# Turning cached keys on VectorE in 32x32 blocks instead of on TensorE, in a two-layer decode kernel

## The chip, the cores and the metric

One core of one Trainium2 chip. The metric is the device time of one execution in microseconds (us), lower is better. A single core has no second die to compare with, so a run is called "slow" here only when it lies more than 1.5% above the fastest run of the same kernel; all others are "fast". Ratios use fast runs alone. "Faster" and "slower" mean by more than 2%; a smaller difference is told with its interval (95%).

## The reference, cut to what matters

Four sequences (B = 4) decode one token each through attention, a gated feed-forward block, and then attention and feed-forward again. Both attention blocks read the same key and value caches, with 32 query heads over 8 cached heads, 4096 positions and a head size of 128, in bf16.

```python
def _A_ref(x, k_cache, v_cache, wq, wo):
    q = ...                                   # (B, 32, 1, 128)
    k = jnp.repeat(k_cache, rep, axis=1)      # rep = 4 query heads per cached head
    v = jnp.repeat(v_cache, rep, axis=1)
    scores = jnp.einsum("bhqd,bhkd->bhqk", q, k) * (Dh ** -0.5)
    p = _softmax(scores, axis=-1)
    o = jnp.einsum("bhqk,bhkd->bhqd", p, v)
    return ... @ wo

x = x + _A_ref(_layernorm(x, axis=-1), A_k_cache, A_v_cache, A_wq, A_wo)
x = x + _B_ref(_layernorm(x, axis=-1), B_w_gate, B_w_up, B_w_down)
x = x + _A_ref(_layernorm(x, axis=-1), A_k_cache, A_v_cache, A_wq, A_wo)
x = x + _B_ref(_layernorm(x, axis=-1), B_w_gate, B_w_up, B_w_down)
```

The kernel walks over the sequences. The turned keys of one sequence stay on chip for both layers ("first pass" and "second pass"); the values are loaded twice.

## The kernel before

A key tile arrives with positions on partitions. The score matmuls of this kernel take them with the head dimension there, so TensorE transposes each 128x128 block with an identity matrix into PSUM, and VectorE or ScalarE copies eight blocks at a time back (`keys`). The score matmuls hold the queries still, in slots padded with zeros so that each of eight key blocks writes its own four of 32 PSUM rows (`scores`). The exponential writes its result in the order in which it reads (`softmax`), and the value matmuls take 4 KB runs of the value cache (`values`).

```python
def keys(b, kvh):
    kt = ktp.tile([P, NKB, NCC, P], BF16, name="kt", tag="kt")     # NKB = 8, NCC = 4
    KT[kvh] = kt
    for t in range(2):
        kn = kvin.tile([P, 2, NKB, Dh], BF16, name="k_t", tag="kv")
        rows = slice(t * CH * P, (t + 1) * CH * P)
        dq.dma_start(out=kn.rearrange("p i k d -> p (i k) d"),
                     in_=A_k_cache[b, kvh, rows].rearrange("(p c) d -> p c d", p=P))
        for hi in range(2):
            tp = ps_tp.tile([P, NKB, P], BF16, name="tp", tag="tp")
            for kb in range(NKB):
                nc.tensor.transpose(tp[:, kb, :], kn[:, hi, kb, :], ident_bf[:, :])
            evac(kt[:, :, 2 * t + hi, :], tp[:])      # 3 of 5 on VectorE, 2 of 5 on ScalarE

def scores(g, zq):
    sc = ps_sc.tile([P, NCC * P], FP32, name="sc", tag="sc")
    for kb in range(NKB):
        for s in range(GH):                            # GH = 4 cached heads in a group
            kvh = g * GH + s
            off = ZW * (kvh + 1) - rep * (kb + 1)
            nc.tensor.matmul(sc[ZW * s:ZW * (s + 1), :], lhsT=zq[:, off:off + ZW],
                             rhs=KT[kvh][:, kb].rearrange("p c k -> p (c k)"), ...)

# in softmax(): maximum over the row (VectorE), over the partitions (GpSimd), then
nc.scalar.activation(out=pr.rearrange("p c k -> p (c k)"), in_=sc[:], func=ACT.Exp,
                     bias=nb[:, 0:1], scale=scale, accum_out=ls[:])

def q_turn(qs, g):                                     # queries of the second pass
    qt = ps_tp.tile([P, rep, P], BF16, name="qt", tag="tp")
    for h in range(rep):
        nc.tensor.transpose(qt[:, h, :], qs[:, h, :], ident_bf[:, :])
    nc.vector.tensor_copy(out=zslots(zq2, g * GH, GH),
                          in_=qt.rearrange("p h (k w) -> p k h w", w=ZW)[:, :, :, 0])

# in values(): two tiles a head, 4 KB runs, then 32 matmuls of 4 columns
dq.dma_start(out=v.rearrange("p i k d -> p (i k) d"),
             in_=A_v_cache[b, kvh, rows].rearrange("(p c) d -> p c d", p=P))
```

The kernel keeps TensorE and the one load queue in the order of the program text. The order around the change from sequence b-1 to b, which the document calls "the turn", is:

```python
        q_turn(qs[0], 0)                     # end of sequence b-1
        sc = scores(0, zq2)
        q_turn(qs[1], 1)
        soft2 = [softmax(sc), softmax(scores(1, zq2))]
        # ... next sequence
        keys(b, 0); prob2 = [turn(soft2[0])]
        keys(b, 1); keys(b, 2); prob2.append(turn(soft2[1])); keys(b, 3)
        soft1 = softmax(scores(0, z1))
        keys(b, 4); keys(b, 5); p1 = [turn(soft1)]
        # ... first value matmuls of sequence b, keys 6 and 7, scores(1, z1), ...
```

## Time and profile before

| kernel before | |
|---|---|
| time, median of 3 runs | 355.69 us (355.35 to 357.77) |
| span of the profiled run | 354.5 us |
| busy: TensorE, VectorE, ScalarE | 247.8, 127.4, 66.0 us |
| transposes of keys / their copies | 75.9 us on TensorE / 51.5 us on VectorE and 52.0 on ScalarE |
| bytes moved by the load queue | 114.58 MB |

No single engine fills the span, so this table does not say what a change is worth. The prediction below reads the stages in which the transfers do not run full. Two groups of the page of the kernel before (name, shapes, count, busy us and mean ns, idle time before them and its cause): the score matmuls and the exponential.

```profile
L304 PE MATMUL sc<-kt,zq 128*32 128x512 bf16 x512 | 37.1, 414 | 5.3 <-DVE zq L204 2.1 <-ACT kt L278 1.9 <-DVE kt L280 1.1
L322 ACT ACTIVATE pr<-sc,nb 128x512 bf16<-128x512 f32 x16 | 11.0, 689 | 97.9 <-DVE am L318 97.9
```

And the granted TensorE clock in 40 slices of the span, in tenths of full speed:

```profile
PEclk9869985555699986556999665556998855587555
```

A 5 is half speed. The 9s are the stages in which keys are turned (1.00 from 175 to 190 us), the 5s mostly those in which four-column value matmuls run (0.50 from 209 to 235). Where a trace has no clock record the row shows 9 too; this one has records from 9.4 us on.

### The profile page before, as it was taken

What the parts mean: (1) busy time and instruction counts of PE and PEld (TensorE: products, weight loads), DVE (VectorE), ACT (ScalarE), POOL (GpSimd) and SP (SyncE); (2) the same over time, 40 slices, a digit from 0 to 9 for tenths busy, and PEclk for the clock granted to TensorE, in tenths of its full rate; (3) what the DMA queues carried; (4) which work ended last, traced back from release to release, by engine and by line L of the source; (5) the groups of instructions that cost most, each with busy time, mean ns of one, the idle gap of its engine ahead of it and who ended that gap; (6) DMA issues with size and microseconds to landing.
All of it is one profiled execution on the core that took longest, in us unless ns stands there. A gap on an engine that the chain in (4) does not pass through costs nothing.

```text
span 354.5 us, 12013 instructions
## 1 busy us (share of the span) xinstructions
PE 247.8 (70%) x5444; PEld 200.6 (57%) x5444; DVE 127.4 (36%) x484; ACT 66.0 (19%) x90; POOL 13.4 (4%) x36
## 2 busy tenths in 40 slices
PE   4578651753888687569887776789886677695465
PEld 4576531643366557555766565755766576644455
DVE  6225330130565421214755120333863303153014
ACT  3215220000064320000545200001652300001000
POOL 0000000000010000000100000000000000001000
PEclk9869985555699986556999665556998855587555
DMA  7998999999459999998699989995799999973940
GB/s 279 411 407 279 349 354 389 407 399 375 184 159 337 329 412 383 409 396 291 197 355 350 410 295 406 408 327 196 232 394 368 392 359 411 383 275 129 398 176 2
DMA packets 35747, 115.34 MB, mean 325 GB/s; under 512 B 3176, under 2 KB 9072, under 8 KB 35696
## 3 DMA queue, kind: packets, MB, share of 16 engines
q1 hardware_dynamic: 35696, 114.58, 86.3%
q8 instruction: 42, 0.69, 0.8%
q14 instruction: 9, 0.07, 0.1%
HBM read 114.56 MB, written 0.00 MB: 323 GB/s over the span
## 4 chain that ended last, share of the span: by engine, by line
DMA 39%; PE 34%; DVE 12%; ACT 6%; issue 5%; POOL 2%; SPq 2%; ACTq 0%; POOLq 0%; DVEq 0%
DMA v_t<-in_A_v_cache_dram 18%; DMA k_t<-in_A_k_cache_dram 10%; PE tp L294 8%; PE sc L304 8%; PE ot L356 7%; DMA wd_sb<-in_B_w_down_dram 6%; DMA wq_sb<-in_A_wq_dram 5%; PE qr L192 4%; ACT kt L278 3%; DVE kt L280 3%; ACT pr L322 3%; PE yT L264 2%; DVE m L311 2%; PE hu L256 1%; SPq L351 1%
## 5 line engine op out<-in xcount | busy, mean ns | idle before, releaser
L356 PE MATMUL ot<-pT,v_t 128*128 128x4 bf16 x2048 | 69.8, 166 | 48.2 <-DMA v_t<-in_A_v_cache_dram 36.8
L356 PEld LDWEIGHTS <-v_t 128*128 128x128 bf16 x2048 | 63.7, 103 | 57.9 <-DMA v_t<-in_A_v_cache_dram 42.0
L294 PE MATMUL tp<-ident_bf,k_t 128*128 128x128 bf16 x1024 | 75.9, 236 | 13.2 <-DMA k_t<-in_A_k_cache_dram 7.5
L294 PEld LDWEIGHTS <-k_t 128*128 128x128 bf16 x1024 | 67.8, 107 | 21.1 <-issue 11.0
L278 ACT COPY kt<-tp 128x1024 bf16<-128x1024 bf16 x52 | 52.0, 1012 | 74.2 <-PE tp L294 74.0
L280 DVE COPY kt<-tp 128x1024 bf16<-128x1024 bf16 x76 | 51.5, 688 | 27.6 <-PE tp L294 27.0
L304 PE MATMUL sc<-kt,zq 128*32 128x512 bf16 x512 | 37.1, 414 | 5.3 <-DVE zq L204 2.1
L361 DVE TENSOR_TENSOR OT_bf<-ot,rden 128x4 bf16<-128x4 f32 x64 | 10.1, 158 | 81.0 <-PE ot L356 80.9
L322 ACT ACTIVATE pr<-sc,nb 128x512 bf16<-128x512 f32 x16 | 11.0, 689 | 97.9 <-DVE am L318 97.9
L304 PEld LDWEIGHTS <-zq 128*32 128x32 bf16 x512 | 14.0, 102 | 21.9 <-issue 6.3
L218 PE MATMUL yT<-OT_bf,wo_sb 128*128 128x1 bf16 (+1 forms) x640 | 21.2, 166 | 1.7 <-issue 1.2
L311 DVE TENSOR_REDUCE m<-sc 128x1 f32<-128x512 f32 x16 | 10.8, 676 | 30.9 <-PE sc L304 30.9
L247 ACT ACTIVATE th<-t 128x14 f32<-128x14 f32 (+1 forms) x5 | 1.1, 222 | 109.7 <-DVE t L245 109.7
L218 PEld LDWEIGHTS <-wo_sb 128*128 128x128 bf16 x640 | 19.5, 104 | 1.9 <-issue 1.9
L316 POOL PARTITION_ALL_REDUCE gm<-am x16 | 6.2, 386 | 284.1 <-DVE am L313 268.8
L192 PE MATMUL qr<-wq_sb,xpad 128*32 128x512 bf16 x128 | 13.9, 612 | 0.6 <-DVE msq L152 0.5
L264 PE MATMUL yT<-H_bf,wd_sb 128*128 128x1 bf16 (+1 forms) x280 | 8.3, 166 | 6.9 <-DMA wd_sb<-in_B_w_down_dram 3.6
L338 PE MATMUL ptp<-ident_bf,pr 128*128 128x128 bf16 x64 | 6.8, 235 | 8.5 <-ACT pr L322 8.0
L264 PEld LDWEIGHTS <-wd_sb 128*128 128x128 bf16 x280 | 8.0, 104 | 7.1 <-DMA wd_sb<-in_B_w_down_dram 3.7
L256 PE MATMUL hu<-xc_bf,wu_sb 128*128 128x1 bf16 (+1 forms) x280 | 8.5, 165 | 4.8 <-DMA wu_sb<-in_B_w_up_dram 2.9
L256 PEld LDWEIGHTS <-wu_sb 128*128 128x128 bf16 x280 | 8.0, 104 | 5.0 <-DMA wu_sb<-in_B_w_up_dram 3.0
L338 PEld LDWEIGHTS <-pr 128*128 128x128 bf16 x64 | 4.5, 103 | 9.7 <-ACT pr L322 8.9
(65 smaller groups left out, 123.6 us busy)
## 6 DMA issues: line engine op xcount, KB each, us to landing
v_t<-in_A_v_cache_dram SPq DMA_DIRECT2D x128, 512.0 KB, 7.0
k_t<-in_A_k_cache_dram SPq DMA_DIRECT2D x64, 512.0 KB, 5.6
wq_sb<-in_A_wq_dram SPq DMA_DIRECT2D x2, 2048.0 KB, 13.0
wo_sb<-in_A_wo_dram SPq DMA_DIRECT2D x1, 4096.0 KB
wg_sb<-in_B_w_gate_dram SPq DMA_DIRECT2D x1, 1792.0 KB, 11.1
wu_sb<-in_B_w_up_dram SPq DMA_DIRECT2D x1, 1792.0 KB, 15.2
wd_sb<-in_B_w_down_dram SPq DMA_DIRECT2D x1, 1792.0 KB, 20.0
x_bf<-in_A_x_dram SPq DMA_DIRECT2D x1, 4.0 KB
```

Source lines behind the costliest of these rows:

```text
L192: nc.tensor.matmul(qr[ZW * j:ZW * (j + 1), :], lhsT=xpad[:, k, :], rhs=wq_sb[:, k, c0:c0 + rep * Dh], start=(k == 0), stop=(k == KD - 1), ...
L218: nc.tensor.matmul(OP["y"][:, :, dk], lhsT=wo_sb[:, i, dk * P:(dk + 1) * P], rhs=o_bf[:, bs, i], start=(i == 0 and dk == 0), stop=(i == Hq ...
L256: nc.tensor.matmul(hu[:, m, :], lhsT=wu_sb[:, k, m * P:(m + 1) * P], rhs=xc_bf[:, bs, k], start=(k == 0), stop=(k == KD - 1))
L264: nc.tensor.matmul(yT[:, :, dk], lhsT=wd_sb[:, k, dk * P:(dk + 1) * P], rhs=H_bf[:, k, :], start=(k == 0), stop=(k == KF - 1))
L278: nc.scalar.copy(out=out_ap, in_=in_ap)
L280: nc.vector.tensor_copy(out=out_ap, in_=in_ap)
L294: nc.tensor.transpose(tp[:, kb, :], kn[:, hi, kb, :], ident_bf[:, :])
L304: nc.tensor.matmul(sc[ZW * s:ZW * (s + 1), :], lhsT=zq[:, off:off + ZW], rhs=KT[kvh][:, kb].rearrange("p c k -> p (c k)"), start=(kb == 0) ...
L311: nc.vector.tensor_reduce(out=m[:], in_=sc[:], axis=AX.X, op=ALU.max)
L322: nc.scalar.activation(out=pr.rearrange("p c k -> p (c k)"), in_=sc[:], func=ACT.Exp, bias=nb[:, 0:1], scale=scale, accum_out=ls[:])
L338: nc.tensor.transpose(ptp[:, cc, :], pr[:, cc, :], ident_bf[:, :])
L356: nc.tensor.matmul(ot[:], lhsT=v[:, hi, kb, :], rhs=pT[:, 2 * t + hi, c:c + rep], start=(t == 0 and hi == 0 and kb == 0), stop=(t == 1 and ...
```

## The change

The intent: take the full transposes, with their two trips through PSUM, away. The new kernel has VectorE transpose within 32x32 blocks directly from SBUF to SBUF. Two bf16 numbers are taken as one four-byte element, so that one instruction turns a whole 512 KB half head (128x1024 elements). What comes out, by the index arithmetic of the code, is not a full transpose: each group of 32 partitions holds 32 of the pairs of head dimensions for its own positions. The queries make up for it: they are spread block-diagonally over the four partition groups (`dsel`, `gmask`, `spread`), so that a score matmul sums only what belongs together. The new order of positions spreads to the rest: the exponential writes with a step of four elements, to bring the positions back into the order that the value matmuls need, and values load in 2 KB runs.

```diff
     def keys(b, kvh):
-        kt = ktp.tile([P, NKB, NCC, P], BF16, name="kt", tag="kt")
+        kt = ktp.tile([P, C, Dh], BF16, name="kt", tag="kt")
+        src = A_k_cache[b, kvh].rearrange("(p a) d -> p a d", p=P)
         for t in range(2):
-            kn = ...; dq.dma_start(...)
-            for hi in range(2):
-                tp = ps_tp.tile([P, NKB, P], BF16, name="tp", tag="tp")
-                for kb in range(NKB):
-                    nc.tensor.transpose(tp[:, kb, :], kn[:, hi, kb, :], ident_bf[:, :])
-                evac(kt[:, :, 2 * t + hi, :], tp[:])
+            kn = kvin.tile([P, CH, Dh], BF16, name="k_t", tag="kv")
+            al = slice(t * CH, (t + 1) * CH)
+            dq.dma_start(out=kn[:], in_=src[:, al])
+            nc.vector.transpose(out=kt[:, al].rearrange("p a d -> p (a d)").bitcast(I32),
+                                in_=kn.rearrange("p a d -> p (a d)").bitcast(I32))
@@ scores
+        for be in range(2):
+            for j in range(NJ):
+                for s in range(GH):
+                    off = (kvh * NJ + j) * ZW + (1 - be) * ZW // 2
+                    kt = KT[kvh].rearrange("p (a b n) (j c o) -> p b j o n a c", a=4, b=2, j=2, o=2)
+                    nc.tensor.matmul(sc[ZW * s:ZW * (s + 1), :], lhsT=zq[:, off:off + ZW],
+                                     rhs=kt[:, be, j // 2, j % 2], ...)
@@ softmax
-        nc.scalar.activation(out=pr.rearrange("p c k -> p (c k)"), in_=sc[:], func=ACT.Exp,
+        nc.scalar.activation(out=pr.rearrange("p n (c a) -> p n a c", a=4),
+                             in_=sc.rearrange("p (n a c) -> p n a c", n=NCC, a=4), func=ACT.Exp,
@@ q_turn
-        nc.vector.tensor_copy(out=zslots(zq2, g * GH, GH), in_=qt.rearrange(...)[:, :, :, 0])
+        qT = grp.tile([P, GH, rep], BF16, name="qT", tag="qT")
+        nc.vector.tensor_copy(out=qT[:], in_=qt.rearrange("p h (k w) -> p k h w", w=ZW)[:, :, :, 0])
+        qz = ps_misc.tile([P, GH, NJ, rep], FP32, name="qz2", tag="misc")
+        for j in range(NJ):
+            nc.tensor.matmul(qz[:, :, j, :], lhsT=dsel[:, j], rhs=qT[:], start=True, stop=True)
+        spread(g * GH, qz.rearrange("p k j h -> p (k j) h"))
@@ values
+        src = A_v_cache[b, kvh].rearrange("(i p l) d -> p i (l d)", i=NI, p=P)
...
+            dq.dma_start(out=v.rearrange("p i b n d -> p i (b n d)"), in_=src[:, 2 * t:2 * t + 2])
```

(Cut: the constants, the same spreading for the first pass, PSUM pools of 3 and 1 buffers that become 2 and 2, a third buffer for the probabilities, the index order in the value matmuls. The order of the stages in the program is unchanged.)

## The prediction

> **What bounds the kernel now.** I read the page first: engine shares, the 40 slices and the queue.
>
> ```profile
> PE 247.8 (70%) x5444; PEld 200.6 (57%) x5444; DVE 127.4 (36%) x484; ACT 66.0 (19%) x90; POOL 13.4 (4%) x36
> ...
> DMA  7998999999459999998699989995799999973940
> GB/s 279 411 407 279 349 354 389 407 399 375 184 159 337 329 412 383 409 396 291 197 355 350 410 295 406 408 327 196 232 394 368 392 359 411 383 275 129 398 176 2
> ...
> q1 hardware_dynamic: 35696, 114.58, 86.3%
> ```
>
> No engine is full; TensorE's 70% counts pipelined matmuls. The hardware queue moves 114.58 MB, and its packets fill 86% of the span. The GB/s row stands near 400 for long stretches and falls in groups of slices: at 88 to 106 us, 159 to 186, 230 to 257 and after 310. At the best rate below, 416 GB/s, the bytes alone take 114.58 / 0.416 = 275 us, so some 80 us are time in which the transfers do not run full. Those holes are what the change can win or widen.
>
> Then the chain that ended last, by engine and by line:
>
> ```profile
> DMA 39%; PE 34%; DVE 12%; ACT 6%; issue 5%; POOL 2%; SPq 2%; ACTq 0%; POOLq 0%; DVEq 0%
> DMA v_t<-in_A_v_cache_dram 18%; DMA k_t<-in_A_k_cache_dram 10%; PE tp L294 8%; PE sc L304 8%; PE ot L356 7%; DMA wd_sb<-in_B_w_down_dram 6%; DMA wq_sb<-in_A_wq_dram 5%; PE qr L192 4%; ACT kt L278 3%; DVE kt L280 3%; ACT pr L322 3%; PE yT L264 2%; DVE m L311 2%; PE hu L256 1%; SPq L351 1%
> ```
>
> Transfers are the largest part, values first. The key path (transposes 8%, their copies out of PSUM 3% on ScalarE and 3% on VectorE) is 14%, about 50 us. That is the most this change could ever take away.
>
> Then stretches of one batch's period (72 to 75 us from one block of query projections to the next): the columns are length, busy time and count per engine, granted TensorE clock, transfer share, GB/s.
>
> ```profile
> 161.00:175.00 14.00, 12.72 (x202) 7.40 (x202) 7.85 (x32) 2.67 (x4) 1.21 (x3) 0.81 0.77 262
> 175.00:190.00 15.00, 12.81 (x213) 10.39 (x211) 10.32 (x23) 9.47 (x13) 1.27 (x3) 1.00 0.96 332
> 190.00:209.00 19.00, 13.25 (x236) 9.77 (x235) 5.66 (x16) 3.83 (x6) 0.83 (x2) 0.78 0.95 361
> 209.00:235.00 26.00, 18.84 (x618) 17.90 (x616) 5.07 (x34) 0.22 (x1) 0.00 (x0) 0.50 0.97 377
> ```
>
> 161 to 175 is the turn from one batch to the next (second-pass queries, two score groups, two softmaxes): 262 GB/s. 175 to 190 turns the next batch's keys. 209 to 235 is the value stretch: 377 GB/s, TensorE at half clock, VectorE 5 of 26 us busy. Only transfers bound that last one.
>
> The turn in order of time, from the chain (start, length, what):
>
> ```profile
> 165.81 0.46 PE qt L203 x4
> 166.30 0.19 DVE zq L204
> ...
> 166.53 1.94 PE sc L304 x32
> 168.49 0.69 DVE m L311
> ...
> 173.47 0.61 PE tp L294 x8
> ...
> 181.47 1.30 DVE kt L280 x2
> ...
> 182.82 1.90 PE sc L304 x29
> ```
>
> After the scores at 166.53, transposes for the new batch wait until the second score group is through, and eight key tiles pass until scores start again at 182.82. Key slots bind them: eight transposed heads are held, all in use until the scores have read them. Six load buffers stand full meanwhile, and the queue has nothing to issue into. So in the turn the transfer rate is the rate at which key tiles are turned.
>
> [...] The trace before has one such operation, the last row here (names, shapes, count, busy us and mean ns):
>
> ```profile
> L280 DVE COPY kt<-tp 128x1024 bf16<-128x1024 bf16 x76 | 51.5, 688 | 27.6 <-PE tp L294 27.0
> ...
> L278 ACT COPY kt<-tp 128x1024 bf16<-128x1024 bf16 x52 | 52.0, 1012 | 74.2 <-PE tp L294 74.0
> ...
> L196 DVE TENSOR_SCALAR qs<-qr,rstd 128x512 bf16<-128x512 f32 x8 | 6.0, 751 | 4.2 <-PE qr L192 4.2
> ...
> L86 DVE STREAM_TRANSPOSE irow<-icol 128x32 f32<-128x32 f32 x1 | 0.2, 205 | 0.0
> ```
>
> [...] a stretch of 1 KB rows (output weights) and one of 4 KB rows (keys and values), both with the transfer share full, ran at
>
> ```profile
> 48.00:55.00 7.00, 0.82 (x13) 0.20 (x5) 1.63 (x7) 0.78 (x2) 0.83 (x2) 0.91 1.09 348
> ...
> 125.00:129.00 4.00, 3.78 (x54) 2.97 (x55) 1.39 (x2) 2.02 (x2) 0.00 (x0) 0.57 1.02 416
> ```
>
> 348 and 416 GB/s. [...] (one score group took 3.61 us at 240.6 and 1.91 at 169.3). The key stretch, 175 to 190, full of transposes, is held at 1.00; without them TensorE will idle there.
>
> **The change part by part.**
>
> Removed: 1024 transposes (75.9 us busy on TensorE) and 128 copies (51.5 us on VectorE, 52.0 on ScalarE).
>
> Added on VectorE: 64 block transposes of 1024 four-byte elements. [...] 1.24 us, an estimate. Sum 79 us. Spreading the queries: a PSUM operation of 512 elements took 751 ns (the qs row), so 0.7 us for each of four batches, and about 0.42 for each of eight half-size ones: 6 us. VectorE goes from 127 to about 127 - 52 + 79 + 6 = 161 us, ScalarE to 14, TensorE to some 175. Averages fit; the question is the turn.
>
> The turn. The instruction order of the new kernel puts a block transpose ahead of the query copy and the maximum of the second group, and others between the softmax steps. From the end of the first scores until eight tiles are turned VectorE must do 8 x 1.24 = 9.9 us plus what stands between: two maxima 1.38, three query operations 1.3, two each of the mask 0.46, the bias 0.5, the row sums 0.48, the reciprocals 0.5 and the probability copies 0.83: 5.5. Together 15.4 us, against 182.82 - 168.47 = 14.4 before. The first tile is free 2.5 us earlier, the eighth about 1 to 2 us later, and tiles 9 to 12 again meet a softmax. VectorE alone replaces three engines that shared the work. Against that, the last key tile of the first layer needs 1.24 us from landing to scores where two blocks of transposes and a 1.02 us copy took 3; but then those scores come after a TensorE pause and run at half clock, 3.5 for 1.9. I call the sum of the key part +0.5 us a period.
>
> Second-pass queries: between the query transposes and the scores there are now a copy, four small matmuls (166 ns of latency each, pipelined, 0.28), another handover and the 0.42 us spread: +0.8 us on the chain in each of four batches. The second group hides behind the first except at the end.
>
> Values. The new key order makes every value run 2 KB instead of 4. Per packet and engine, 16 x 4096 B / 416 GB/s = 157 ns and 16 x 1024 / 348 = 47; a straight line gives 84 ns at 2048 B, 391 GB/s, so a value tile takes 1.34 us for 1.26. All 128 would pay 10 us; where the chain hangs on value landings (about 20 tiles a batch, 210.7 to 226.2 and part of the projections after) it is about 1.7 us a batch. Key runs keep 4 KB.
>
> Sum: three turns at 0.5 + 0.8 + 1.7 = 3.0 make 9. The first batch adds 1 for its scores at half clock (its opening is held by weight transfers until 20.2 us anyway), and the tail 0.8 + 0.4 + 1.2 for queries and values, 3.4 together. That is +12. Since TensorE's in-order queue loses 76 us of work that also delayed value matmuls, which I cannot place on the chain, I take 3 back: 355.7 + 9 = 365.
>
> **The rivals.** (a) The handovers were the bound. If most of the 50 us of the key path vanishes behind landings, 330 to 342. For it: in the queue's own waits, 54.8 us of key loads stood until transposes freed a buffer. Against: in the turn a VectorE tile (1.24 us) is no faster than what TensorE and two copy engines did (14.4 us for eight with the softmaxes in it). (b) Transfers hide everything: the value stretches are 35% of the span and neither kernel changes their bytes; 353 to 359. Against: the packets shrink. (c) [...] 2.3 us a tile, 147 us in all; VectorE would be the bound in the key stretches, +10 us for eight tiles in each turn, 390 to 400. [...] (d) The packets cost in full, near 10 us by themselves, with the turn unchanged: 366.
>
> **Range and chances.** 365 us, 350 to 379 eight times in ten: the lower end lets a third of (a) through beside half of my costs, the upper end allows the full packet cost and 2 us more in each turn. Two per cent are 348.6 and 362.8. Faster 0.20, for the handovers; same 0.33, because the changes are single microseconds in both directions; slower 0.47.
>
> **What would show it.** The block transposes' mean: 1.2 to 1.3 us is my step, over 2 is rival (c). Value stretches with full transfer share: 391 GB/s is the packet step, 410 refutes it. From the end of a batch's second-pass scores to the next batch's first: 15 to 17 us is the turn step; under 12 and I am wrong, since VectorE then overlaps better than its order suggests. Score groups of the first layer at 3.5 us would confirm the clock. ScalarE near 14 and VectorE near 161 us check the counts. If the GB/s row fills in the turn slices and the total falls below 345, rival (a) holds.

The 1.24 us of a block transpose and the 2.3 us of rival (c) are estimates. The trace before, with one block transpose of 32 columns in 205 ns, does not show either.

## The result, and the profile after

| | before | after |
|---|---|---|
| median of 3 runs | 355.69 us | 368.15 us (366.34 to 369.49) |
| ratio of fast runs | | 1.033 (95%: 1.024 to 1.042) |
| profiled span | 354.5 us | 366.3 us |

The change makes the kernel slower by 3.3%. Ratios here and below are the mean time of one kernel's fast runs over that of the other's in the same rounds, so not quite the ratio of the medians quoted.

The page of the changed kernel, with the rows that answer to those shown of before: engines, clock, transfers, queue, and the chain that ended last by engine and by line.

```profile
PE 195.3 (53%) x4468; PEld 140.3 (38%) x4468; DVE 155.0 (42%) x483; ACT 24.8 (7%) x38; POOL 13.4 (4%) x36
...
PEclk9999999999965655555956555558665555586555
DMA  7999799999358999999698999997899999963940
GB/s 276 411 401 355 234 349 375 389 399 379 140 173 267 340 364 330 369 385 350 212 351 319 360 352 362 385 314 262 300 378 326 379 346 385 357 226 119 385 179 4
...
q1 hardware_dynamic: 52080, 114.58, 87.0%
...
DMA 34%; PE 28%; DVE 22%; ACT 7%; issue 6%; POOL 2%; SPq 1%; ACTq 0%; POOLq 0%; DVEq 0%
DMA v_t<-in_A_v_cache_dram 24%; PE sc L320 10%; DVE kt L307 9%; PE ot L374 7%; ACT pr L339 6%; DMA wd_sb<-in_B_w_down_dram 6%; DMA k_t<-in_A_k_cache_dram 4%; PE qr L211 4%; PE yT L287 2%; DVE m L328 2%; POOL den L346 1%; DVE zq L145 1%; PE hu L279 1%; PE st L158 1%; DVE pT L358 1%
```

TensorE lost 52.5 us of busy time and ScalarE 41.2; VectorE gained 27.6. The bytes are the same but the packets are smaller (52080 for 35696). In the chain the transposes and their copies (14% before) have become block transposes (9%), values have grown from 18% to 24%, scores from 8% to 10% and the exponential from 3% to 6%. The clock row needs care. Its first eleven 9s say nothing: this trace has no clock record before 100.9 us, and the two score groups there (23.6 to 31.2 and 47.7 to 51.3 us) have medians of 632 and 628 ns a matmul, as at half clock. From the 12th slice on the row has far fewer 9s than before: the scores' growth has its reason in the clock. For the same cause the mean granted clock of a whole run is not compared here.

The groups concerned:

```profile
L307 DVE STREAM_TRANSPOSE kt<-k_t 128x1024 int32<-128x1024 int32 x64 | 77.5, 1227 | 16.4 <-DMA k_t<-in_A_k_cache_dram 8.4 <-PE sc L320 7.9
...
L320 PE MATMUL sc<-kt,zq 128*32 128x512 bf16 x512 | 52.0, 534 | 18.8 <-DVE kt L307 13.9 <-DVE zq L145 4.8
L339 ACT ACTIVATE pr<-sc,nb 128x512 bf16<-128x512 f32 x16 | 22.4, 1401 | 191.2 <-DVE am L335 144.6 <-DVE OT_bf L379 46.6
...
L145 DVE TENSOR_TENSOR zq<-qz,gmask 128x256 bf16<-128x256 f32 x8 | 3.3, 418 | 1.5 <-PE qz L228 1.3
...
L145 DVE TENSOR_TENSOR zq<-qz,gmask 128x512 bf16<-128x512 f32 x4 | 2.7, 675 | 0.0
```

A block transpose takes 1.23 us. The score matmuls are the same 512 instructions of the same shape as before and take 534 ns where they took 414. Over single matmuls the shortest is 376 ns in both kernels, and the median went from 379 to 628 ns: more of them run at half clock (the group at 208.34 us was granted 0.50 and took 3.56 us, that at 174.01 was granted 1.00 and took 2.01; with 378 and 630 ns for the two kinds, the means come to 14% of them before and 62% after). The new layout of their moving operand adds little: a second-pass group of 32 at full clock took 1.99 to 2.03 us where it took 1.91. The exponential of 128x512 takes 1401 ns for 689. Nothing in the prediction had that.

The turn of the changed kernel in order of time, from the chain (start us, length us, engine and line):

```profile
173.53 0.44 DVE zq L145
...
174.01 2.01 PE sc L320 x26
...
176.08 1.13 issue
177.21 0.13 DVE qT L225
177.35 0.60 DVE m L328
...
178.42 1.15 DVE kt L307
...
187.70 2.28 DVE kt L307 x2
...
190.02 3.39 PE sc L320 x27
...
193.44 0.69 DVE m L328
...
196.73 1.41 ACT pr L339 x2
...
199.62 1.01 PE ot L374 x32
...
200.65 0.16 DVE OT_bf L379
200.81 1.16 DVE kt L307
201.99 5.71 DMA v_t<-in_A_v_cache_dram
...
208.34 3.56 PE sc L320 x32
```

To read it: the first second-pass scores end at 176.03, the copy of the second queries waits 1.13 us for a block transpose that stands ahead of it in VectorE's order, and block transposes then follow each other to the next sequence's scores at 190.02. That is 14.0 us, against 14.35 before (168.47 to 182.82). The key part of the turn has not become longer. But then the first scores take 3.39 for 1.90 us, the maximum and its successors stand between further block transposes, and the exponential takes 1.41: the first value matmul of the new sequence comes at 199.62, 23.6 us after the same starting point, where it came after 21.4 us before (168.47 to 189.89). The line at 208.34 is the second group of first-layer scores, 3.56 us.

What that does to the transfers, in windows cut at the same events (length, busy time and count of TensorE, weight loads, VectorE, ScalarE, GpSimd, then granted clock, transfer share, GB/s). Before:

```profile
168.50:182.80 14.30, 11.91 (x207) 9.60 (x205) 10.10 (x26) 7.53 (x10) 1.65 (x4) 1.00 0.75 243
182.80:189.90 7.10, 6.33 (x98) 4.78 (x99) 4.46 (x11) 4.52 (x6) 0.83 (x2) 1.00 1.03 381
189.90:197.00 7.10, 4.85 (x108) 4.25 (x108) 2.31 (x5) 1.15 (x3) 0.00 (x0) 1.00 0.96 368
```

After, with a value stretch as the last line:

```profile
176.00:190.00 14.00, 5.74 (x91) 3.04 (x88) 13.44 (x27) 2.80 (x4) 1.66 (x4) 0.74 0.78 269
190.00:199.60 9.60, 3.99 (x33) 1.62 (x33) 6.16 (x11) 1.39 (x2) 0.83 (x2) 0.68 0.99 355
199.60:208.30 8.70, 2.49 (x84) 2.37 (x87) 4.98 (x6) 0.00 (x0) 0.00 (x0) 0.50 0.86 303
222.00:233.00 11.00, 6.93 (x201) 6.35 (x202) 2.70 (x19) 0.00 (x0) 0.00 (x0) 0.50 1.04 385
```

In the turn (first lines) the rates are 243 and 269 GB/s, VectorE is busy 13.44 of 14 us after the change, and the clock has fallen from 1.00 to 0.74. Up to the first value matmul (second lines) the queue still fills buffers, 381 and 355 GB/s. Then comes the hole: 199.6 to 208.3 moves 303 GB/s where the same place before moved 368, TensorE is busy 2.49 of 8.7 us, and the chain there says why: it waits 5.71 us for a value tile that was issued at 201.99, when a block transpose had freed a load buffer; this transpose stood in VectorE's order behind the scaling of the first outputs (`OT_bf`, 200.65), which needs the late first value matmuls. Where values run full (last line), they run at 385 GB/s with a transfer share over 1.

### The profile page after: what moved, and what is told of

It is laid out like the page before. It is cut to its first block, busy times and chain, and to the rows that moved or that the text cites.

```text
span 366.3 us, 10014 instructions
## 1 busy us (share of the span) xinstructions
PE 195.3 (53%) x4468; PEld 140.3 (38%) x4468; DVE 155.0 (42%) x483; ACT 24.8 (7%) x38; POOL 13.4 (4%) x36
## 2 busy tenths in 40 slices
DMA packets 52123, 115.22 MB, mean 315 GB/s; under 512 B 3176, under 2 KB 9072, under 8 KB 52080
## 3 DMA queue, kind: packets, MB, share of 16 engines
q1 hardware_dynamic: 52080, 114.58, 87.0%
## 4 chain that ended last, share of the span: by engine, by line
DMA 34%; PE 28%; DVE 22%; ACT 7%; issue 6%; POOL 2%; SPq 1%; ACTq 0%; POOLq 0%; DVEq 0%
DMA v_t<-in_A_v_cache_dram 24%; PE sc L320 10%; DVE kt L307 9%; PE ot L374 7%; ACT pr L339 6%; DMA wd_sb<-in_B_w_down_dram 6%; DMA k_t<-in_A_k_cache_dram 4%; PE qr L211 4%; PE yT L287 2%; DVE m L328 2%; POOL den L346 1%; DVE zq L145 1%; PE hu L279 1%; PE st L158 1%; DVE pT L358 1%
## 5 line engine op out<-in xcount | busy, mean ns | idle before, releaser
L307 DVE STREAM_TRANSPOSE kt<-k_t 128x1024 int32<-128x1024 int32 x64 | 77.5, 1227 | 16.4 <-DMA k_t<-in_A_k_cache_dram 8.4
L320 PE MATMUL sc<-kt,zq 128*32 128x512 bf16 x512 | 52.0, 534 | 18.8 <-DVE kt L307 13.9
L339 ACT ACTIVATE pr<-sc,nb 128x512 bf16<-128x512 f32 x16 | 22.4, 1401 | 191.2 <-DVE am L335 144.6
L320 PEld LDWEIGHTS <-zq 128*32 128x32 bf16 x512 | 16.7, 118 | 43.5 <-issue 33.2
L356 PE MATMUL ptp<-ident_bf,pr 128*128 128x128 bf16 x64 | 9.1, 291 | 39.2 <-ACT pr L339 39.2
L328 DVE TENSOR_REDUCE m<-sc 128x1 f32<-128x512 f32 x16 | 10.9, 683 | 26.5 <-PE sc L320 26.5
L343 DVE TENSOR_SCALAR lm<-onehot,ls 128x16 f32<-128x16 f32 x16 | 3.7, 231 | 16.4 <-ACT pr L339 16.3
L200 PE MATMUL qps<-xc_bf,wq_sb 128*128 128x4 bf16 x128 | 3.7, 168 | 11.6 <-DMA wq_sb<-in_A_wq_dram 11.6
L260 PE MATMUL hg<-xc_bf,wg_sb 128*128 128x1 bf16 (+1 forms) x280 | 8.2, 165 | 2.6 <-DMA wg_sb<-in_B_w_gate_dram 2.2
L260 PEld LDWEIGHTS <-wg_sb 128*128 128x128 bf16 x280 | 8.1, 105 | 2.8 <-DMA wg_sb<-in_B_w_gate_dram 2.2
```

Of the source, the lines that this page charges most:

```text
L260: nc.tensor.matmul(hg[:, m, :], lhsT=wg_sb[:, k, m * P:(m + 1) * P], rhs=xc_bf[:, bs, k], start=(k == 0), stop=(k == KD - 1))
L307: nc.vector.transpose(out=kt[:, al].rearrange("p a d -> p (a d)").bitcast(I32), in_=kn.rearrange("p a d -> p (a d)").bitcast(I32))
L328: nc.vector.tensor_reduce(out=m[:], in_=sc[:], axis=AX.X, op=ALU.max)
L339: nc.scalar.activation(out=pr.rearrange("p n (c a) -> p n a c", a=4), in_=sc.rearrange("p (n a c) -> p n a c", n=NCC, a=4), func=ACT.Exp, ...
L356: nc.tensor.transpose(ptp[:, cc, :], pr[:, cc, :], ident_bf[:, :])
```

## The experiments

Three theories of the 3.3%: (1) the exponential's strided write, about 0.7 us for each of 16 softmaxes; (2) the value runs of 2 KB; (3) score groups at half clock, 3.56 us each for 1.90 (that this comes of TensorE having less to do before them is a guess). The rival to all of them is the new part itself: VectorE's block transposes and the longer path of the queries, now in one engine's order.

Each kernel ran beside the kernel before on the same chip; there were three calls on three chips, of 5, 3 and 5 rounds. The changed kernel itself ran again only in the first, so what the second and third say against it is a comparison across chips. Kernels marked "wrong" compute something else; they still passed the tolerance, since with these inputs attention is nearly uniform over 4096 positions. That the kernels called correct are so rests on the index arithmetic of their code.

| kernel | ratio to before, 95% | median us | before |
|---|---|---|---|
| changed kernel again (after_again) | 1.036 (1.031 to 1.041) | 367.30 | 354.35 |
| exponential written in order (exp_flat) | 1.020 (1.010 to 1.030) | 364.34 | 354.35 |
| values in 4 KB runs (v_4k) | 1.024 (1.018 to 1.029) | 363.18 | 354.35 |
| filler matmuls (pe_warm) | 1.060 (1.055 to 1.066) | 375.10 | 354.35 |
| first-layer scores halved (score_half) | 1.020 (1.006 to 1.033) | 362.18 | 358.64 |
| short query path (query_short) | 1.031 (1.017 to 1.044) | 366.52 | 358.64 |
| three undone (three_undone) | 0.989 (0.977 to 1.000) | 351.53 | 358.64 |
| exponential reads strided (exp_read) | 1.025 (1.013 to 1.037) | 364.81 | 358.64 |
| before, 2 KB values (before_v2k) | 1.014 (1.009 to 1.019) | 358.42 | 354.33 |
| before, strided exponential (before_exp) | 1.023 (1.017 to 1.030) | 363.45 | 354.33 |
| mended | 1.025 (1.019 to 1.032) | 363.26 | 354.33 |
| mended_more | 1.011 (1.006 to 1.016) | 357.63 | 354.33 |

The medians are of all runs, the ratios of the fast ones. In the second call three of the seven runs of the kernel before were slow; with all runs counted the four ratios of that call would be 0.006 to 0.009 lower.

### The changed kernel again

No edit; it is the baseline.

> The changed kernel once more, as the yardstick on the same chip as its variants. Ratio to the kernel before 1.03, between 1.024 and 1.042 as first measured; about 366 to 369 us.

It was 3.6% slower than before, in line with the first measurement.

### Exponential written in order (wrong)

```diff
-        out=pr.rearrange("p n (c a) -> p n a c", a=4),
-        in_=sc.rearrange("p (n a c) -> p n a c", n=NCC, a=4), func=ACT.Exp,
+        out=pr.rearrange("p n x -> p (n x)"), in_=sc[:], func=ACT.Exp,
```

> The changed kernel, but the exponential writes its 512 probabilities in the order in which it reads them, so that they land in the wrong columns and the result is wrong on purpose. The profile has the exponential at 1.40 us where the kernel before had 0.69, 16 times. Theory 1 (the strided write is what slows it, and it lies on the chain, which my prediction left out): 0.69 us again and 8 to 11 us less in total, ratio about 1.00 to 1.01. Rival (it waits in slack behind the block transposes or the landings of values): 0.69 us but 3 us or less off the total, ratio 1.025 or more. If the exponential stays at 1.4 us, it was not the write.

The exponential went back to 688 ns. The fast runs are 1.6% of before, some 5.7 us, below the changed kernel. But only two of its six runs count as fast, since one of 358.86 us makes the 1.5% limit narrow; the profiled run is among the others. All six together average 364.2 us against 367.2 for the changed kernel, a gain of 3.0. So the direction holds and the size is 3 to 6 us, below the 8 to 11 that theory 1 expected and at or above the 3 of its rival.

### Values in 4 KB runs (wrong)

```diff
-        src = A_v_cache[b, kvh].rearrange("(i p l) d -> p i (l d)", i=NI, p=P)
+        src = A_v_cache[b, kvh].rearrange("(t p x) d -> p t (x d)", t=2, p=P)
...
-            dq.dma_start(out=v.rearrange("p i b n d -> p i (b n d)"), in_=src[:, 2 * t:2 * t + 2])
+            dq.dma_start(out=v.rearrange("p i b n d -> p (i b n d)"), in_=src[:, t])
```

> The changed kernel, but the value loads take 4 KB runs as before; the values meet the wrong probabilities, so the result is wrong on purpose. Theory (my packet step): packets of 4 KB at 159 ns in place of two of 84 ns, value stretches back from 388 to about 410 GB/s, 5 to 8 us less in total, ratio 1.010 to 1.018. Rival (the loads have slack): 2 us or less.

A value stretch of this kernel, in the same columns as above:

```profile
226.00:236.00 10.00, 6.72 (x234) 6.48 (x234) 2.44 (x17) 0.21 (x1) 0.00 (x0) 0.50 1.03 406
```

406 GB/s with a full transfer share, for 385 after the change. In the records of the two traces a packet takes 159 ns at 4 KB and 84 ns at 2 KB (medians), so 2 KB cost 168 where 4 KB cost 159. The time fell by 1.25% of before, 4.4 us, a little under the 5 to 8 expected; the interval of the difference leaves 2 to 7.

### Filler matmuls to hold the clock

After each block transpose, three matmuls of 512 columns on the tile just turned, into a PSUM tile that nobody reads.

```diff
+            dum = ps_misc.tile([P, 512], FP32, name="dum", tag="misc")
+            for j in range(3):
+                nc.tensor.matmul(dum[0:ZW, :], lhsT=dsel[:, 0, 0:ZW],
+                                 rhs=kt[:, t * CH + 4 * j:t * CH + 4 * j + 4].rearrange("p a d -> p (a d)"),
+                                 start=True, stop=True)
```

> The changed kernel with three matmuls of 512 columns into an unread PSUM tile after each block transpose, so that TensorE stays busy while VectorE turns keys; result right. Theory (the half clock of the first layer's scores is on the chain): those scores go from 3.56 to about 1.9 us, 8 groups save up to 13 us of which I expect 4 to 8 in the total, ratio 1.010 to 1.02. Rival (scores hide behind landings, or the filler itself delays the value matmuls): total unchanged or up, ratio 1.03 or more.

The score matmuls' median fell from 628 to 403 ns, so with the filler most of them ran near the 378 ns of full clock. But the kernel is 2.4% slower than the changed one. The chain of this kernel has the filler itself on it:

```profile
205.31 2.74 PE dum L311 x6
...
211.50 1.07 PE dum L311 x3
```

The fillers waited 19.9 us in all for VectorE's block transposes, and the value matmuls that follow them in TensorE's order began only when they had ended (208.05 and 212.58 us). The loads in turn wait for buffers that value matmuls free (79.5 us of value loads in the changed kernel). So this run shows that with work on TensorE just ahead most scores were fast (the eight first-layer groups were busy 23.0 us together, for 32.5 in the changed kernel), and nothing of what that is worth in time: it is inconclusive for theory 3.

### First-layer scores halved (wrong)

Instead of raising the clock, this takes half of the 32 matmuls out of each first-layer score group, so that a group at half clock lasts about as long as a full one at full clock (1.90 us in the kernel before).

```diff
-    def scores(g):
+    def scores(g, halves=2):
-        for be in range(2):
+        for be in range(halves):
-        soft1 = softmax(scores(0))   # and scores(1)
+        soft1 = softmax(scores(0, 1))   # and scores(1, 1); cut: the stop flag follows halves
```

> The changed kernel, but in the first layer each score group runs only 16 of its 32 matmuls (the second half of the keys is left out, so the result is wrong on purpose). At half clock a group then takes about 1.8 us, as 32 matmuls did at full clock in the kernel before, without the filler that spoiled the last test. Theory (the half clock of eight score groups is on the chain): 3 to 8 us less than the changed kernel, ratio 1.014 to 1.028. Rival (scores hide behind landings): under 2 us, ratio over 1.03.

Two groups of the first layer on its chain took 1.88 and 1.83 us. All score matmuls together:

```profile
L320 PE MATMUL sc<-kt,zq 128*32 128x512 bf16 x384 | 38.6, 501 | 18.2 <-DVE kt L307 13.3 <-DVE zq L145 4.8
```

The ratio to before is 1.020 where the changed kernel had 1.036: 1.7% of before, 5.9 us, across chips; the two intervals together leave 1 to 11. Theory 3 stands with a rough size, though its rival (under 2 us) is not quite excluded. In the traces the eight first-layer groups were busy 20.0 us in the kernel before, 32.5 in the changed one and 19.6 here: the halving takes off about what the clock had added.

### Short query path (wrong)

The second pass copies its turned queries straight into place, without the four matmuls and the spread.

```diff
-        qT = ...; nc.vector.tensor_copy(out=qT[:], in_=qt...)
-        qz = ...; 4 x nc.tensor.matmul(qz..., lhsT=dsel[:, j], rhs=qT[:])
-        spread(g * GH, qz.rearrange("p k j h -> p (k j) h"))
+        dst = bass.AP(zq.tensor, zq[:, lo:].offset, [zq[:, lo:].ap[0], [NJ * ZW, GH], [1, rep]])
+        nc.vector.tensor_copy(out=dst, in_=qt.rearrange("p h (k w) -> p k h w", w=ZW)[:, :, :, 0])
```

> The changed kernel, but in the second pass the queries are copied straight from the transposes into the score weights, as before, without selecting matmuls and spread (wrong on purpose). My step said 0.8 us for each of four batches and 0.4 at the tail: 3 to 4 us less, ratio 1.025 to 1.029. Rival (the first query step is hidden by value matmuls in between): under 1.5 us, ratio over 1.032.

In the trace the step from the copy of the queries to the scores took 0.22 us (95.88 to 96.10) instead of 0.98. In time it is 1.031 for 1.036 across chips, a difference of 2 us with an interval of some 5 us to each side: not resolved.

### The three undone together (wrong)

exp_flat, v_4k and score_half in one kernel: what stays of the change is the block transposes, the spread queries, and the buffers.

> The plain exponential, the 4 KB values and the half scores together (wrong on purpose). If the three are separate serial costs, their sum of 5.8 + 4.4 + about 5 us comes off: 351 to 354, ratio 0.995 to 1.005. If they share the same slack, or the block transposes set the pace once the others are gone, it stays at 357 or more, ratio 1.01 or over.

0.989, and its upper limit only just reaches 1. The single effects, taken off the changed kernel's 1.036, give 1.036 - 0.016 - 0.0125 - 0.0166 = 0.991. So the three add up, and they account for the whole slowdown: the rest of the change, its costs and its gains taken together, costs nothing that these runs can see, and may be worth about 1%. That it is a real gain is not shown.

### Exponential that reads with a step and writes in order (correct)

The reordering can be put on the input: the same elements, in the order of the output.

```diff
-        out=pr.rearrange("p n (c a) -> p n a c", a=4),
-        in_=sc.rearrange("p (n a c) -> p n a c", n=NCC, a=4), func=ACT.Exp,
+        out=pr.rearrange("p n (c a) -> p n c a", a=4),
+        in_=sc.rearrange("p (n a c) -> p n c a", n=NCC, a=4), func=ACT.Exp,
```

> The changed kernel with the result right: the exponential writes its row in order and instead reads PSUM with a step of 32 elements. If only the strided write is slow, 0.69 us each and a total as in the flat run, 358 to 364, ratio about 1.02. If ScalarE pays for steps on either side, about 1.4 us again and ratio 1.03 to 1.04.

```profile
L339 ACT ACTIVATE pr<-sc,nb 128x512 bf16<-128x512 f32 x16 | 11.0, 687 | 194.9 <-DVE am L335 163.0 <-DVE OT_bf L379 31.9
```

The same 16 exponentials take 687 ns. Reading PSUM with a step of 32 elements cost nothing here (687 ns for 689 in the kernel before); it is the write with a step of four bf16 elements that doubles the time (1401 ns). In time the kernel stands at 1.025 for 1.036 across chips, about 4 us less, with an interval that reaches 0. Anyone who keeps the change should take this form; the results stay right.

### The two simple costs put into the kernel before (wrong)

```diff
# before_v2k
-                in_=A_v_cache[b, kvh, rows].rearrange("(p c) d -> p c d", p=P))
+                in_=A_v_cache[b, kvh, rows].rearrange("(i p l) d -> p i (l d)", i=2, p=P))
# before_exp
-        nc.scalar.activation(out=pr.rearrange("p c k -> p (c k)"), in_=sc[:], func=ACT.Exp,
+        nc.scalar.activation(out=pr.rearrange("p n (c a) -> p n a c", a=4),
+                             in_=sc.rearrange("p (n a c) -> p n a c", n=NCC, a=4), func=ACT.Exp,
```

> The kernel before, but with values in two 2 KB runs per partition and load (they meet the wrong probabilities). The mirror of the 4 KB test: if the packet cost belongs to value streams as such, 4 to 5 us more, ratio 1.010 to 1.016; if it only shows beside the block transposes, under 1.006.

It took 1.4% longer, 5.0 us (interval 3.2 to 6.8). The 4.4 us of v_4k come back from the other side.

> The kernel before, but its exponential writes with the step of four elements, as in the changed kernel (probabilities in the wrong columns). The exponential goes from 0.69 to 1.40 us; if it lies on the chain there too, 5 to 8 us more, ratio 1.013 to 1.023; it may cost more here, since ScalarE also copies transposed keys in this kernel. Under 1.006 would say that only the changed kernel has it on the chain.

```profile
L322 ACT ACTIVATE pr<-sc,nb 128x512 bf16<-128x512 f32 x16 | 22.5, 1406 | 98.8 <-DVE am L318 98.8
```

The exponential took 1406 ns here too, and the kernel took 2.3% longer, 8.2 us (interval 6.0 to 10.5). This is the cleanest number for theory 1: the write step alone, with nothing else of the change, is worth most of the 22.5 - 11.0 = 11.5 us that it adds. In the changed kernel taking it away gave less, 3 to 6 us. If this and before_v2k add up (they were not run together), the two make 3.7%, all of the slowdown before any half clock is counted; so the change must win some time back elsewhere.

### Mended: strided reads, and scores in two column halves (correct)

Two ideas to win the change back: exp_read, and first-layer scores computed for the first half of every head as soon as those halves are turned, so that only half a group at low clock stands at the end.

```diff
-    def keys(b, kvh):
+    def keys(b, kvh, halves=(0, 1)):
-    def scores(g):
+    def scores(g, parts=1):
+        for h, be, j, s in [(h, be, j, s) for h in range(parts) for be in range(2) for j in range(NJ) for s in range(GH)]:
+            nc.tensor.matmul(o[:, :, h * na:(h + 1) * na], lhsT=zq[:, off:off + ZW],
+                             rhs=kt[:, be, j // 2, j % 2, :, h * na:(h + 1) * na], ...)
-        soft1 = softmax(scores(0))
+        soft1 = softmax(scores(0, 2))   # cut: the first halves of the keys are loaded and turned before the second; exp_read's edit
```

> The changed kernel with a right result and two mends: the exponential reads PSUM in steps and writes in order, and the first layer's score groups run in two halves by key column, with the key tiles loaded half by half, so that the first half is computed while the last tiles are still turned. If the costs are separate, 4 to 6 us for the exponential and 3 to 6 for the scores come off 1.036: ratio 1.005 to 1.015, about 358 to 360. If the reordered loads cost what the early scores win, 1.02 or more.

1.025 where 1.005 to 1.015 was expected, and the same as exp_read alone, across chips: the halves won nothing that can be seen. Three steps of its chain:

```profile
170.16 3.53 PE sc L322 x26
...
195.02 1.01 PE ot L376 x32
...
205.69 3.56 PE sc L322 x58
```

At the turn they did what they should: from the end of the second-pass scores (173.69) to the first value matmul (195.02) it is 21.3 us, for 22.5 in the same turn of exp_read (in the other two turns 23.5 for 22.1 and 21.5 for 23.3). But at 205.69 the second group runs its halves in one piece, 3.56 us as ever: TensorE had been waiting for a value tile (7.66 us from 197.39) that its order puts first, so the first halves were not done ahead. And in this run the second-pass scores ahead of the turn took 3.53 us (first line), as groups at half clock do, where in exp_read they took 2.01. The split could help here only where TensorE's order let the first part go first.

### Mended more: three small copies on ScalarE as well (correct)

mended, and in the turn the copy of the queries and the two copies of the turned probabilities move from VectorE to ScalarE, which has little to do after the change (24.8 us busy).

```diff
-        nc.vector.tensor_copy(out=qT[:], in_=qt...)
+        nc.scalar.copy(out=qT[:], in_=qt...)
-            prob2 = [turn(soft2[0])]              # and prob2.append(turn(soft2[1]))
+            prob2 = [turn(soft2[0], nc.scalar.copy)]
```

> The mended kernel with ScalarE, which is 93% idle, doing the query copy of the second pass and the two probability copies of the turn in place of VectorE. If VectorE sets the pace of the turn, about 1 us in each of three turns: 0.005 to 0.01 less than the mended kernel, ratio near 1.00. If the copies on ScalarE (slower per instruction) only lengthen the handover, no gain, within 0.004 of it.

```profile
170.07 0.18 ACT qT L225
...
171.06 2.05 PE sc L322 x22
...
179.44 5.99 DMA k_t<-in_A_k_cache_dram
...
186.72 6.52 DMA k_t<-in_A_k_cache_dram
```

357.63 us, 1.011: 1.4% better than mended, more than expected of three copies. The query copy no longer waits behind a block transpose (TensorE waits 0.32 us for the second one, at 173.74), the first second-pass scores take 2.05 us, as at full clock, in two of the three turns (in the first turn they took 3.56 us), and from 179.44 the chain hangs on landing keys. From the end of the first second-pass scores to the next sequence's first value matmul, the three turns of the traces take:

| kernel | three turns, us |
|---|---|
| before | 21.4, 21.4, 22.2 |
| changed | 23.2, 23.6, 23.5 |
| mended | 23.5, 21.3, 21.5 |
| mended_more | 21.6, 18.9, 19.1 |

So mended_more's turns are 6.7 us shorter in sum than mended's, which is of the order of the time gained (5.1 us by the fast runs' means); this is one trace each. In all three turns of mended_more the two halves of the first score group ran as one piece of 64 matmuls (in the second from 183.19 to 186.69 us), so no first half was computed ahead. The turns are also shorter than those of the kernel before, 59.6 us in sum for 65.0: what still makes the kernel slower lies outside them, the 2 KB values among it. It is the best form of the changed kernel that was found. It still takes 1% longer than the kernel before (interval 0.6 to 1.6). No version that computes the right thing beat it.

## Why the prediction was right or wrong

The prediction was 365 us in 350 to 379, with slower as the likeliest outcome; 368.15 us and 3.3% slower came out. The total was right, several of its terms were not, and they partly cancelled: a cost that was left out (the exponential) stands against turns that were priced too high and time that the change won back. That the total fell in the middle of the range is in part luck.

- Block transpose: 1.24 us predicted, an estimate that no trace had shown; 1.227 mean measured. Rival (c), 2.3 us, is out, though only this one size was run. VectorE: 161 us predicted, 155.0 measured.
- Value packets: 84 ns and 391 GB/s predicted, 84 ns and 385 GB/s measured. At 1.7 us a batch and 1.2 at the tail the sum held some 6 us for them; v_4k measured 4.4 and before_v2k 5.0. Right, slightly large. In the two traces loads with a full transfer share ran at 348 GB/s in 1 KB rows, 385 in 2 KB and 395 to 416 in 4 KB. Rival (d), the full 10 us, is out.
- Clock of the first-layer scores: 3.5 us predicted, 3.56 measured, so the half clock came as predicted. Its cost did not: the prediction folded it into a net +0.5 us per turn and +1 in the first batch, and score_half put it near 6 us, with a wide interval. What was missed is where the half clock acts: these scores stand ahead of the first value matmuls, on which the freeing of load buffers hangs, directly and through VectorE's order (the value tile issued at 201.99 us).
- The cause of the half clock: the prediction expects it for scores that come after a pause of TensorE. That was not shown. The two durations that it gives, 3.61 and 1.91 us, show that there are two rates, not that idling is the cause: ahead of the group at 240.6 TensorE ran query projections for 3.59 us without a break, and from 209 to 235 it was busy for 18.84 of 26 us at a granted clock of 0.50. In the same kernel TensorE ran nothing but transposes of keys from 23.1 to 28.0 us, and the clock went from 0.50 to 1.00 (0.50 from 22.0 to 26.4, 1.00 from 26.5 to 28.0); later 6 us in which they filled 4.59 (176 to 182) were granted 1.00. What lowers the clock here is not shown.
- The turn: 15 to 17 us predicted for the key part, 14.0 measured, 14.35 before. That lies between the prediction and its own sign of being wrong (under 12). VectorE does fill the turn, as predicted (13.44 of 14 us). The sum of VectorE's instructions at their single durations was too long: back to back, block transposes follow 1.13 us apart (188.77, 189.89 and 191.02) and the maximum adds 0.60. So the added turn time of this step is not there up to the first scores; three_undone shows that block transposes, queries and buffers together cost nothing that can be seen.
- The exponential: left out. The diff shows the strided write, and the prediction put ScalarE at 14 us; it came to 24.8, because each of 16 exponentials takes 1401 instead of 689 ns. This is the step that failed most clearly: worth 3 to 6 us in the changed kernel, 8.2 in the kernel before.
- TensorE: 175 us predicted, 195.3 measured. The score groups account for 52.0 - 37.1 = 14.9 of the 20, since they run at half clock.
- Queries: +0.8 us per batch predicted; from the copy of the queries to the scores the trace shows 0.99 us (173.02 to 174.01) for 0.23, so +0.76. Right as a step; its worth in time stays open.
- The 3 us taken back for TensorE's relieved queue: the remainder of the change after the three undone costs is at 0.989, which would fit a gain of that order, but its interval touches no gain at all.
- Rival (a), that the handovers had been the bound: the turn's rate rose only from 243 to 269 GB/s, so at most a small part of it is true. Rival (b), transfers hiding everything, falls with the result: the costs showed in the total.

What stays open: the clean size of the clock's effect (warming TensorE disturbed its order, halving changes the work), what the longer query path costs in time, what of the 1.4% of mended_more is the copies themselves and what the clock that comes with them, and whether these copies do the same without the split scores.

## What to carry to other kernels

A layout change is paid for where the new order is undone (in the kernel before, 8.2 us for the write with a step and 5.0 for the 2 KB values): follow it through to every write with a step and every run that gets shorter, and price those before the part that the change is about. If the order must be changed inside a PSUM-to-SBUF instruction, try it on the read side (the exponential here took 687 ns with the step on the read, 1401 with it on the write). With work taken off TensorE the matmuls on the critical path ran at a lower clock here (first-layer scores: 20.0 us busy before, 32.5 after; the cause is not shown), and work gathered on one engine delayed what is small and stood behind it in its order (the copy of the second queries waited 1.13 us for a block transpose): try the small copies on the engine that has been relieved (mended_more, 1.4% less than mended).
